# Local attention and a squared-ReLU layer on one core: bias put into the score banks first, masks made at the start, two more tiles transposed by DMA

## The chip, the cores and the metric

The kernel runs on one core of a Trainium2 chip. The metric is device time in microseconds (us) of one launch; several runs are taken and their median is compared. One execution is also recorded by the hardware profiler; its views show each engine's instructions by start time and line of the kernel, counted from the first instruction. Engines: PE (TensorE, matmuls; PEld is its weight load), ACT (ScalarE), DVE (VectorE), POOL (GpSimd), SP (SyncE). POOL and SP start transfers (DMA); their queues are called POOLq and SPq.

## The reference

Attention over 4 batches of 8 heads, 768 positions, head size 64. Each position sees the 96 latest positions, itself included, and the first 8 ("global") ones. A linear bias by distance, with a slope for each head, is added. The result goes through a two-layer network.

```python
scores = scale * np.matmul(q, k.transpose(0, 1, 3, 2))
rel = pos[:, None] - pos[None, :]
is_global = pos[None, :] < int(n_global)              # 8
is_local = (rel >= 0) & (rel < int(n_local))          # 96
dist = np.where(is_global & ~is_local, float(n_local), np.abs(rel))
scores = np.where(is_global | is_local, scores - slopes * dist, -1e9)
a = softmax(scores);  x = a @ v       # x: 3072 rows, 8 heads * 64 = 512 columns
h = x @ w_in                          # 512 -> 2048
out = np.maximum(h, 0.0) ** 2 @ w_out # 2048 -> 512
```

## The kernel before, in words

**Tiles.** The 3072 rows are 24 tiles of 128 rows (index `j`), six to a batch. Because 96 is less than 128, a tile attends to itself and to the tile before it; the eight global keys and values are copied into the first rows of the neighbour (L524 for k, L595 for v). The first tile of a batch attends only to itself. Two tiles are a block of the network (12 blocks).

**Attention of a tile.** q and k arrive with rows on the partitions and must be transposed. For tiles 0 to 5 PE does it (L376; tile 0 in fp32, since it is loaded by SP without a cast, the others in bf16), and ACT or DVE copies the result from PSUM (L305 or L307, whichever the planner picks). From tile 6 on (`JQK`) a DMA transpose on SP does it (L400). Scores are matmuls of L435 with 64 rows of weights. How bias and mask come in depends on the tile. For tiles 0 to 2 (`NBIAS`), PE adds them by further matmuls into the same PSUM banks, after the scores (L447): the weights are identities scaled by the head's slope (`sid`), the moving operand is a 128 x 256 table of distances and masks (`pb`, for first tiles `pb0`). ACT then takes the exponential of the banks (L483). From tile 3 on ACT takes the exponential of the bare scores, and DVE multiplies it by a precomputed mask `E` (L508; `E0` for the first tile of a batch), which ACT makes as exp(slope * pb) by eight instructions of L313. L550 multiplies by v; DVE divides by the row sums (L577, L578) and leaves `x`. x has to be transposed for the network: up to tile 5 by PE (L613) and a copy (L305 or L307), from tile 6 on (`JX`) by a DMA transpose on SP (L637), which waits for x.

**Network.** A block has eight steps. Step s: `hT` = w_in slice times x transposed (L661, 8 matmuls), ACT's ReLU (L682), DVE's square (L694, 14 buffers), then two sums into the two accumulator banks (L731, 2 matmuls each). After eight steps the sums are copied out and stored by SP (L766).

**Constants.** DVE clears a zero tile and writes ones; POOL makes position differences `pbi` by an iota (L244); DVE derives two identities (L255, L256), `pbt`, `pbw`, `pb` (L259 to L265), eight `sid` (L267), then `pb0` and the rows of global keys (L270 to L274). PE runs eight matmuls on zeros first (L254).

**Loads.** POOL issues nearly all loads (L193), with a cast to bf16, in a fixed order: q of tile 1, k of tile 1, v of tiles 0 and 1, then tiles 2 to 5 among the sixteen slices of w_in and w_out. Tiles from 6 on are loaded into two buffers by turns, when the transpose of the tile two before has freed them.

**Order.** Everything after the constants is an operation of a planner (class `Plan`): it has a cost for each engine that could do it, dependencies, a key (lower goes first among operations that can start at about the same time), and may take buffers of a ring. `run` simulates the engines with these costs and `LAG` (the time from the end of an operation until another engine can use its result) and emits the instructions in the order of the simulated starts. On the chip each engine then keeps that order and waits where data is not there. Six PSUM banks are such a ring (`G`): transposes, scores, `hT` and most products with v take its banks in turn; an operation that takes a bank waits until the users of that bank, six allocations ago, have finished.

Of the kernel before, what the change touches and what calls it, by code (L numbers as in the profile page):

```python
# [11 lines left out]
FP32 = mybir.dt.float32  # L12
# [9 lines left out]
class Plan:  # L22
# [8 lines left out]

    LAG = {"PE": 0.25, "ACT": 0.15, "DVE": 0.12, "SP": 2.6, "POOLQ": 0.8, "DMAQ": 1.2, "DMA": 0.0}
    URGE = 0.05
# [66 lines left out]
def kernel(  # L100
# [36 lines left out]
    NBIAS = 3  # L137
    JQK, JX = 6, 6
    NQ, NKT = 2, 2 * TPB
# [32 lines left out]
    NHS = 14  # L172
    E_AT = 14.0
    NWARM = 8
# [65 lines left out]
    nc.vector.memset(zero.bitcast(I32), 0)  # L240
    for j in range(NFIRST + 2):
        nc.vector.memset(v_sb[j][:, :, D : D + 1], 1.0)
    load_part(0, 1)
    nc.gpsimd.iota(pbi, pattern=[[-P, 2], [-1, P]], base=0, channel_multiplier=1)  # L244
    issue[0] += 0.4
    load_part(1, 1)
# [6 lines left out]
    for i in range(NWARM):  # L253
        nc.tensor.matmul(out=warm, lhsT=zero[:, :P], rhs=zero, start=True, stop=True)  # L254
    nc.vector.tensor_scalar(ident32, pbi[:, 0, :], 0.0, None, op0=Alu.is_equal)  # L255
    nc.vector.tensor_scalar(ident, pbi[:, 0, :], 0.0, None, op0=Alu.is_equal)  # L256

# [5 lines left out]
        pbw, pbi, float(n_local - 1), -MASK_VAL, op0=Alu.add, op1=Alu.mult  # L263
    )
    nc.vector.tensor_tensor(out=pb, in0=pbt, in1=pbw, op=Alu.min)  # L265
    for h in range(H):
        nc.vector.tensor_scalar_mul(sid[h], ident, float(slopes[h] / scale))  # L267

    def emit_pb0(e):
        nc.vector.tensor_copy(pb0, pb[:, 0, :])  # L270
        nc.vector.tensor_scalar_max(
            pb0[:n_global, :], pb0[:n_global, :], float(-n_local)
        )
        nc.vector.memset(pb[:n_global, 1, :], float(-n_local))  # L274

    pb_op = plan.op(("pb",), {"DVE": 0.75}, emit_pb0, key=-40.0)

    def emit_ones(e, js):
        for j in js:
            nc.vector.memset(v_sb[j][:, :, D : D + 1], 1.0)  # L280

# [21 lines left out]
    def any_copy(e, dst, src):  # L303
        if e == "ACT":
            nc.scalar.copy(dst, src)  # L305
        else:
            nc.vector.tensor_copy(dst, src)  # L307

    maskE = [
        plan.op(  # L310
            ("E", odd, g), {"ACT": 0.8}, key=0.3 + 2 * g + odd, ready=E_AT,
            emit=lambda e, odd=odd, g=g: [
                nc.scalar.activation(  # L313
                    E[:, odd, g, i], pb, Act.Exp, scale=float(slopes[4 * g + 2 * i + odd])
                )
                for i in range(2)
            ],
        )
        for g in range(2)
        for odd in range(2)  # L320
    ]

    def emit_E0(e, odd):
# [7 lines left out]
        plan.op(  # L331
            ("E0", odd), {"DVE": 0.6}, emit=lambda e, odd=odd: emit_E0(e, odd), key=9 + odd,
            deps=[maskE[odd], maskE[2 + odd]],
        )
# [11 lines left out]
    for j in range(NT):  # L346
# [22 lines left out]
        for n in range(2) if j < JQK else ():  # L369
            users = []  # L370

            def emit_tr(e, j=j, n=n, fp=fp):
                tr = ps_g.tile([P, NPAIR, P], FP32 if fp else BF16, name="tr", tag="g")
                src = plain[n, j] if fp else qk_ring[slot(j)][:, n, :]
                for pair in range(NPAIR):
                    nc.tensor.transpose(  # L376
                        out=tr[:, pair, :], in_=src[:, pair * P : (pair + 1) * P],
                        identity=ident32 if fp else ident,
                    )
                tiles["tr", n, j] = tr  # L380

            tr = plan.op(
                ("tr", n, j), {"PE": 0.5 if fp else 0.24}, emit_tr,
                deps=[land["qk"[n], j]], key=base, takes=(*G, [users]),
            )

            def emit_T(e, j=j, n=n, T_=T_):
                any_copy(e, T_[:, n], tiles.pop(("tr", n, j)))

            c = plan.op(  # L390
                ("T", n, j), {"DVE": 0.7 if fp else 0.43, "ACT": 0.57}, emit_T,
                deps=[tr] + ku, key=base + 0.1,
            )
            users += [tr, c]
            parts.append(c)
            if not fp:
                qk_users[slot(j)].append(tr)
# [20 lines left out]

        def emit_sc(e, gs, j=j, first=first):
            sc = {}  # L420
            for g in gs:
                for odd in range(2):
                    sc[odd, g] = ps_g.tile([P, 4, P], FP32, name="sc", tag="g")
                    tiles["sc", j, odd, g] = sc[odd, g]
            todo = [
                (0, pair, pair, 0) if first else (pair // 2, pair, 2 * (pair % 2) + kt, kt)
                for pair in range(NPAIR)
                for kt in range(1 if first else 2)
            ]
            todo = [x for x in todo if x[0] in gs]  # L430
            opened = set()
            for g, pair, at, kt in todo:
                for odd in range(2):
                    half = slice(odd * D, (odd + 1) * D)
                    nc.tensor.matmul(  # L435
                        out=sc[odd, g][:, at, :],
                        lhsT=qkT[(j - kt) % NKT][half, 1, pair, :],
                        rhs=qkT[j % NKT][half, 0, pair, :],

                        start=j >= NBIAS or (odd, g) not in opened,  # L440
                        stop=j >= NBIAS,
                        skip_group_check=True,
                    )
                    opened.add((odd, g))
            for g, pair, at, kt in todo if j < NBIAS else ():
                for odd in range(2):
                    nc.tensor.matmul(  # L447
                        out=sc[odd, g][:, at, :],
                        lhsT=sid[2 * pair + odd],
                        rhs=pb0 if first else pb[:, kt, :],  # L450
                        start=False,
                        stop=True,
                        skip_group_check=True,
                    )

        deps = list(parts)
        if j < NBIAS:
            deps.append(pb_op)
        if not first:
            deps += tiles["kready", j - 1] + [glob.get(("k", j - 1))]  # L460
        s_ = {}
        for gs in [(0,), (1,)] if j < NSPLIT and not first else [tuple(range(groups))]:
            n = 8 * len(gs)
            o = plan.op(
                ("sc", j, gs[0]), {"PE": 0.25 + 0.029 * n + (0.056 * n if j < NBIAS else 0)},
                lambda e, gs=gs, f=emit_sc: f(e, gs), deps=deps, key=base + 1 + 2 * gs[0],
                takes=(*G, busers[2 * gs[0] : 2 * gs[-1] + 2]),
            )
            ku.append(o)
            if not first:  # L470
                kT_users[(j - 1) % NKT].append(o)
            s_.update({g: o for g in gs})
        for g in range(groups):
            for odd in range(2):
# [3 lines left out]
                def emit_exp(e, j=j, odd=odd, g=g):  # L478
# [10 lines left out]
                x_ = plan.op(  # L489
                    ("exp", j, odd, g), {"ACT": 0.58}, emit_exp, deps=[s_[g]],  # L490
                    key=base + 1.1 + 2 * g + odd,
                    takes=("at", 8, [musers]) if j < NBIAS else ("esc", 3, [eusers]),
                )
                users += [s_[g], x_]
                if j < NBIAS:
# [5 lines left out]
                def emit_mul(e, j=j, odd=odd, g=g, first=first):  # L501
# [9 lines left out]
                m_ = plan.op(  # L511
                    ("mul", j, odd, g), vec(0.38), emit_mul,
                    deps=[x_, maskE0[odd] if first else maskE[2 * g + odd]],
                    key=base + 1.2 + 2 * g + odd, takes=("at", 8, [musers]),
# [7 lines left out]
        if 1 <= t < TPB - 1:  # L522
            def emit_gk(e, j=j, t=t):
# [4 lines left out]
            glob["k", j] = plan.op(  # L528
                ("gk", j), vec(0.17), emit_gk, deps=list(s_.values()), key=base + 4
            )  # L530
# [6 lines left out]
        for hf in range(2):  # L537
# [34 lines left out]
            def emit_norm(e, j=j, hf=hf):  # L572
# [12 lines left out]
            n_ = plan.op(  # L585
                ("norm", j, hf), vec(0.6), emit_norm,
                deps=[p_] + norm, key=base + 2.3 + 2 * hf,
# [5 lines left out]
        if 1 <= t < TPB - 1:  # L593
            def emit_gv(e, j=j, t=t):
                nc.vector.tensor_copy(v_sb[j][:n_global], v_sb[j - t][:n_global])  # L595

            glob["v", j] = plan.op(
                ("gv", j), vec(0.28), emit_gv, deps=[p_, norm[1]], key=base + 5
            )
# [6 lines left out]
        if j < JX:  # L606
# [22 lines left out]

            c = plan.op(("xT", j), {"DVE": 0.43, "ACT": 0.57}, emit_xT, deps=[f_], key=base + 5.1, takes=xT_ring)  # L630
            users += [f_, c]
# [22 lines left out]
    for n, (blk, s) in enumerate(order1):  # L654
# [30 lines left out]
        rusers = []  # L685
        r = plan.op(("relu", blk, s), {"ACT": 0.58}, emit_relu, deps=[a], key=n + 0.5, takes=("hr", 2, [rusers]))
        users.append(r)
# [8 lines left out]

        d = plan.op(("sq", blk, s), vec(0.68), emit_sq, deps=[r], key=n + 1.0, takes=("hs", NHS, [husers]))
        rusers.append(d)
# [10 lines left out]
    for blk in range(NBLK):  # L709
# [9 lines left out]
        for s, sub, half in order2:  # L719
# [29 lines left out]
            if s == NSTEP - 1:  # L749
                ousers = []  # L750

                def emit_o(e, blk=blk, sub=sub, half=half, cols=cols):
# [4 lines left out]
                ev = plan.op(  # L757
                    ("o", blk, sub), {"ACT": 0.57, "DVE": 0.62} if half is None else {"ACT": 0.37},
                    emit_o, deps=[o], key=8 * blk + s + 1.0, takes=("o", 4, [ousers]),
# [16 lines left out]

    for o in plan.run({"PE": 4.2, "DVE": 4.4, "ACT": 4.2, "DMAQ": issue[1]}):
        if o["emit"]:
            o["emit"](o["engine"])
# [35 lines left out]
```

## Time and profile before

| What | Value |
|---|---|
| median of 5 runs | 216.15 us (215.5 to 216.94) |
| the profiled execution: its time / its span | 216.94 us / 215.1 us |
| last matmul ends | 212.0 us |
| PE / DVE / ACT / POOL busy | 206.1 / 142.0 / 118.8 / 73.9 us |
| granted TensorE clock | 1.000 |
| idle of PE before its first matmul | 1.19 us |
| PE busy from 7.7 to 15.6 us | 6.73 of 7.90 us |
| PE busy from 15.6 to 28.1 us | 11.35 of 12.50 us |
| PE busy from 28.1 to 68.7 us | 40.54 of 40.60 us |
| PE busy from 68.7 to 212.0 us | 142.37 of 143.30 us |
| packet time of POOL's load queue / of SP's queue, share of 16 DMA engines | 84.0% / 33.9% |

A line of a timeline gives the start, the duration, the engine, the line of the kernel, the output and inputs, the shape and the count, and in brackets the idle time of the engine just before it with what ended it. A line of the waits gives the waiting instruction, what it waited for, the total in us, the number of waits and the longest. PE's matmuls overlap in the pipeline, so the time a group costs is read from one start to the next.

### The profile page before, as it was taken

Reading aid. Unit: us, or ns where it says so; the run is one execution under the profiler, and the core shown is the slowest. Engines: PE = TensorE matmul, PEld = TensorE weight load, DVE = VectorE, ACT = ScalarE, POOL = GpSimd, SP = SyncE. Lnnn points to the kernel's source line nnn. Section 1 sums busy time; section 2 is a strip of 40 time slices with the busy share of each in tenths; the row PEclk is TensorE's granted clock in tenths of the full one; section 3 lists DMA queues with packets and bytes.
Section 4 is the critical chain, followed back from the end, with each engine's and each line's share of the span. In section 5 each row is a group of like instructions: output and inputs, shape, how many; then the busy total and the mean of one; then the engine's idle time right before and its main releaser. Section 6 shows DMA issues by size and latency. Waiting matters only on the chain.

```text
span 215.1 us, 5031 instructions
## 1 busy us (share of the span) xinstructions
PE 206.1 (96%) x1992; PEld 141.4 (66%) x1992; DVE 142.0 (66%) x366; ACT 118.8 (55%) x218; POOL 73.9 (34%) x91
## 2 busy tenths in 40 slices
PE   7689999999998999999999999999999999999994
PEld 3576567657665767666767667666767767766773
DVE  5287967735687668657778768666767767755540
ACT  2598675714574735733845745733746746734431
POOL 7996677309044440408143140408112000000000
PEclk9999999999999999999999999999999999999999
DMA  9999999999999999799969959999999810310202
GB/s 127 151 163 198 181 195 184 175 215 108 163 190 111 195 137 118 136 144 96 149 147 117 160 117 118 148 125 108 198 127 84 174 24 3 122 24 3 98 0 98
DMA packets 113702, 27.58 MB, mean 128 GB/s; under 512 B 104336, under 2 KB 110736, under 8 KB 113680
## 3 DMA queue, kind: packets, MB, share of 16 engines
q0 software_dynamic: 79200, 13.37, 84.0%
q1 hardware_dynamic: 34480, 13.90, 33.9%
q8 instruction: 15, 0.25, 0.5%
q14 instruction: 7, 0.06, 0.1%
HBM read 27.26 MB, written 6.29 MB: 156 GB/s over the span
## 4 chain that ended last, share of the span: by engine, by line
PE 66%; DMA 23%; POOL 7%; issue 2%; ACT 0%; POOLq 0%; DVE 0%; SPq 0%
PE hT L661 30%; PE acc L731 29%; DMA qk<-in_k_dram 8%; DMA qkT<-qk 5%; DMA win<-in_moe_w_in_dram 4%; DMA wout<-in_moe_w_out_dram 4%; PE sc L435 4%; POOL qk L193 3%; PE po L550 3%; DMA xT<-x 2%; POOL v L193 2%; POOL win L193 1%; POOL wout L193 1%; ACT o L305 0%; POOL pbi L244 0%
## 5 line engine op out<-in xcount | busy, mean ns | idle before, releaser
L661 PE MATMUL hT<-xT,win 128*128 128x256 bf16 x768 | 99.0, 273 | 1.8 <-DMA xT<-x 0.9
L731 PE MATMUL acc<-wout,hs 128*128 128x512 bf16 (+1 forms) x400 | 95.6, 370 | 0.1
L682 ACT ACTIVATE hr<-hT 128x512 f32<-128x512 f32 x96 | 57.3, 598 | 61.6 <-PE hT L661 60.1
L661 PEld LDWEIGHTS <-win 128*128 128x128 bf16 x768 | 70.9, 98 | 19.9 <-DMA win<-in_moe_w_in_dram 1.6
L694 DVE TENSOR_TENSOR hs<-hr 128x512 bf16<-128x512 f32 x96 | 65.0, 689 | 25.5 <-ACT hr L682 24.8
L731 PEld LDWEIGHTS <-hs 128*128 128x128 bf16 x400 | 38.5, 98 | 27.8 <-DVE hs L694 0.2
L483 ACT ACTIVATE esc<-sc 128x512 bf16<-128x512 f32 x78 | 42.6, 598 | 13.2 <-PE sc L435 13.1
L193 POOL DMA_DIRECT2D qk<-in_q_dram x23 | 20.7, 899 | 82.2 <-DMA qkT<-qk 80.0
L508 DVE TENSOR_TENSOR at<-esc,E 128x512 bf16<-128x512 bf16 x78 | 32.4, 420 | 6.9 <-ACT esc L483 5.8
L193 POOL DMA_DIRECT2D v<-in_v_dram x24 | 21.6, 900 | 2.0 <-DVE at L508 1.2
L578 DVE TENSOR_TENSOR x<-po,rs 128x256 bf16<-128x256 f32 x48 | 20.4, 424 | 1.7
L193 POOL DMA_DIRECT2D qk<-in_k_dram x23 | 20.7, 900 | 1.5 <-DMA v<-in_v_dram 1.3
L550 PEld LDWEIGHTS <-at 128*128 128x128 bf16 x352 | 16.7, 98 | 5.8 <-ACT at L483 0.4
L550 PE MATMUL po<-v,at 128*128 128x65 bf16 x352 | 18.7, 193 | 0.3 <-ACT at L483 0.3
L435 PEld LDWEIGHTS <-qkT 64*128 64x128 bf16 x352 | 9.9, 94 | 9.9 <-issue 8.3
L577 DVE RECIPROCAL rs<-po 128x4 f32<-128x4 f32 x48 | 8.7, 181 | 9.7 <-PE po L550 9.6
L435 PE MATMUL sc<-qkT 64*128 64x128 bf16 x192 | 13.2, 219 | 1.0 <-DVE qkT L307 0.5
L305 ACT COPY o<-acc 128x512 f32<-128x512 f32 (+1 forms) x14 | 7.8, 557 | 9.2 <-PE acc L731 9.2
L307 DVE COPY o<-acc 128x512 f32<-128x512 f32 x11 | 7.6, 692 | 7.2 <-PE acc L731 7.2
L435 PE MATMUL sc<-qkT,qkT 64*128 64x128 bf16 x160 | 11.4, 216 | 0.0
L524 DVE COPY qkT<-qkT 128x32 bf16<-128x32 bf16 x16 | 3.6, 227 | 7.4 <-PE sc L435 7.3
L193 POOL DMA_DIRECT2D win<-in_moe_w_in_dram x8 | 6.5, 811 | 0.6 <-DMA wout<-in_moe_w_out_dram 0.6
(40 smaller groups left out, 60.4 us busy)
## 6 DMA issues: line engine op xcount, KB each, us to landing
out_dram<-o SPq DMA_DIRECT2D x23, 256.0 KB, 3.7
v<-in_v_dram POOLq DMA_DIRECT2D x24, 128.0 KB, 6.4
qk<-in_q_dram POOLq DMA_DIRECT2D x23, 128.0 KB, 4.9
qk<-in_k_dram POOLq DMA_DIRECT2D x23, 128.0 KB, 5.7
win<-in_moe_w_in_dram POOLq DMA_DIRECT2D x8, 256.0 KB, 8.5
wout<-in_moe_w_out_dram POOLq DMA_DIRECT2D x8, 256.0 KB, 8.8
qkT<-qk SPq DMA_TRANSPOSE x18, 5.0
xT<-x SPq DMA_TRANSPOSE x18, 3.1
```

The costliest lines, as they stand in the source:

```text
L193: nc.gpsimd.dma_start(out=dst, in_=src)
L305: nc.scalar.copy(dst, src)
L435: nc.tensor.matmul(out=sc[odd, g][:, at, :], lhsT=qkT[(j - kt) % NKT][half, 1, pair, :], rhs=qkT[j % NKT][half, 0, pair, :],  start=j >= N ...
L483: nc.scalar.activation(out=esc, in_=tiles.pop(("sc", j, odd, g)).rearrange("p a c -> p (a c)"), func=Act.Exp, scale=scale,)
L508: nc.vector.tensor_mul(at, tiles.pop(("esc", j, odd, g)), bias)
L550: nc.tensor.matmul(out=po[:, hi, :], lhsT=tiles["at", j, odd, g][:, at * P : (at + 1) * P], rhs=v_sb[kj][:, h, :], start=(i == 0), stop=(i ...
L577: nc.vector.reciprocal(rs, po[:, :, D : D + 1])
L578: nc.vector.tensor_tensor(out=x[:, 4 * hf : 4 * hf + 4, :], in0=po[:, :, :D], in1=rs.to_broadcast([P, 4, D]), op=Alu.mult,)
L661: nc.tensor.matmul(out=hT[:, c, :], lhsT=w_in_sb[s][:, kt, c * P : (c + 1) * P], rhs=tiles["xT", blk][:, kt, :], start=(kt == 0), stop=(kt ...
L682: nc.scalar.activation(hr, tiles.pop(("hT", blk, s)), Act.Relu)
L694: nc.vector.tensor_mul(hs, hr, hr)
L731: nc.tensor.matmul(out=tiles["acc", blk, sub, half], lhsT=hs[:, c, sub * P : (sub + 1) * P], rhs=w_out_sb[s][:, c, cols], start=(s == 0 an ...
```

## The change

1. *Bias first.* For tiles 0 to 2 the bias matmuls become an operation of their own (`bias`). It depends on the tile's second transpose (`tr`, that of k), takes the PSUM banks and opens them (`start`); the scores depend on it and add to the banks.
2. *Constants.* The iota goes ahead of POOL's first load. The identities move behind `pbt` and `pbw`; `pb0` and the rows of global keys come before the `sid`, outside the planner. The eight instructions that make `E` on ACT come right after these, before everything that the planner orders; before, they were four operations of the planner, not to start before 14 us of its time. `E0` then waits for nothing but a planned time of 8.0.
3. *x by DMA.* `JX` goes from 6 to 4: x of tiles 4 and 5 is transposed on SP too, so 20 tiles instead of 18.
4. *The planner's numbers.* Lags of ACT and DVE, the costs of many operations, and the times at which engines are free at the start.

```diff
-    LAG = {"PE": 0.25, "ACT": 0.15, "DVE": 0.12, "SP": 2.6, "POOLQ": 0.8, "DMAQ": 1.2, "DMA": 0.0}
+    LAG = {"PE": 0.25, "ACT": 0.26, "DVE": 0.2, "SP": 2.6, "POOLQ": 0.8, "DMAQ": 1.2, "DMA": 0.0}
...
-    JQK, JX = 6, 6
+    JQK, JX = 6, 4
...
-    E_AT = 14.0
...
+    nc.gpsimd.iota(pbi, pattern=[[-P, 2], [-1, P]], base=0, channel_multiplier=1)
     load_part(0, 1)
-    nc.gpsimd.iota(pbi, pattern=[[-P, 2], [-1, P]], base=0, channel_multiplier=1)
-    issue[0] += 0.4
     load_part(1, 1)
...
-    nc.vector.tensor_scalar(ident32, pbi[:, 0, :], 0.0, None, op0=Alu.is_equal)
-    nc.vector.tensor_scalar(ident, pbi[:, 0, :], 0.0, None, op0=Alu.is_equal)
...
+    nc.vector.tensor_scalar(ident32, pbi[:, 0, :], 0.0, None, op0=Alu.is_equal)
+    nc.vector.tensor_scalar(ident, pbi[:, 0, :], 0.0, None, op0=Alu.is_equal)
     nc.vector.tensor_tensor(out=pb, in0=pbt, in1=pbw, op=Alu.min)
+
+    nc.vector.tensor_copy(pb0, pb[:, 0, :])
+    nc.vector.memset(pb[:n_global, 1, :], float(-n_local))
+    nc.vector.tensor_scalar_max(pb0[:n_global, :], pb0[:n_global, :], float(-n_local))
     for h in range(H):
         nc.vector.tensor_scalar_mul(sid[h], ident, float(slopes[h] / scale))
...
+    for g in range(2):
+        for odd in range(2):
+            for i in range(2):
+                nc.scalar.activation(
+                    E[:, odd, g, i], pb, Act.Exp, scale=float(slopes[4 * g + 2 * i + odd])
+                )
...
-            ("E0", odd), {"DVE": 0.6}, emit=lambda e, odd=odd: emit_E0(e, odd), key=9 + odd,
-            deps=[maskE[odd], maskE[2 + odd]],
+            ("E0", odd), {"DVE": 0.62}, emit=lambda e, odd=odd: emit_E0(e, odd), key=9 + odd,
+            ready=8.0,
...
-                ("T", n, j), {"DVE": 0.7 if fp else 0.43, "ACT": 0.57}, emit_T,
+                ("T", n, j), {"DVE": 0.61 if fp else 0.41, "ACT": 0.48}, emit_T,
...
+        def emit_bias(e, gs, j=j, first=first, todo=todo, open_sc=open_sc):
+            open_sc(gs)
             opened = set()
+            for g, pair, at, kt, odd in todo(gs):
+                nc.tensor.matmul(
+                    out=tiles["sc", j, odd, g][:, at, :],
+                    lhsT=sid[2 * pair + odd],
+                    rhs=pb0 if first else pb[:, kt, :],
+                    start=(odd, g) not in opened,
+                    stop=False,
+                    skip_group_check=True,
+                )
+                opened.add((odd, g))
+
+        def emit_sc(e, gs, j=j, todo=todo, open_sc=open_sc):
+            if j >= NBIAS:
+                open_sc(gs)
+            for g, pair, at, kt, odd in todo(gs):
+                half = slice(odd * D, (odd + 1) * D)
+                nc.tensor.matmul(
+                    out=tiles["sc", j, odd, g][:, at, :],
+                    lhsT=qkT[(j - kt) % NKT][half, 1, pair, :],
+                    rhs=qkT[j % NKT][half, 0, pair, :],
+                    start=j >= NBIAS,
+                    stop=True,
+                    skip_group_check=True,
+                )
...
+            takes = (*G, sc_users)
+            bias = None
+            if j < NBIAS:
+                bias = plan.op(
+                    ("bias", j, gs[0]), {"PE": 0.056 * n},
+                    lambda e, gs=gs, f=emit_bias: f(e, gs), deps=[tr],
+                    key=base + 0.9 + 2 * gs[0], takes=takes,
+                )
+                takes = None
             o = plan.op(
-                ("sc", j, gs[0]), {"PE": 0.25 + 0.029 * n + (0.056 * n if j < NBIAS else 0)},
-                lambda e, gs=gs, f=emit_sc: f(e, gs), deps=deps, key=base + 1 + 2 * gs[0],
-                takes=(*G, busers[2 * gs[0] : 2 * gs[-1] + 2]),
-            )
+                ("sc", j, gs[0]), {"PE": 0.2 + 0.029 * n},
+                lambda e, gs=gs, f=emit_sc: f(e, gs), deps=[*deps, bias],
+                key=base + 1 + 2 * gs[0], takes=takes,
+            )
...
-                    ("exp", j, odd, g), {"ACT": 0.58}, emit_exp, deps=[s_[g]],
+                    ("exp", j, odd, g), {"ACT": 0.48}, emit_exp, deps=[s_[g]],
...
-        d = plan.op(("sq", blk, s), vec(0.68), emit_sq, deps=[r], key=n + 1.0, takes=("hs", NHS, [husers]))
+        d = plan.op(("sq", blk, s), vec(0.61), emit_sq, deps=[r], key=n + 1.0, takes=("hs", NHS, [husers]))
...
-    for o in plan.run({"PE": 4.2, "DVE": 4.4, "ACT": 4.2, "DMAQ": issue[1]}):
+    for o in plan.run({"PE": 4.2, "DVE": 4.2, "ACT": 5.3, "DMAQ": issue[1]}):
```

`open_sc` takes the PSUM tiles of the scores; `todo` lists a tile's score matmuls by group, pair of heads, place, key tile and head of the pair. Further costs change in the same way: ReLU from 0.58 to 0.48, the mask's product from 0.38 to 0.34, the division from 0.6 to 0.55, the copies of k's and v's global rows from 0.17 to 0.1 and 0.28 to 0.25, the copies of the sums from 0.57 and 0.62 to 0.48 and 0.61.

## The prediction

> **What bounds the kernel now.** I read the times first: the profiled execution took 216.94 us around a span of 215.1 us, so 1.84 us lie outside the span. The median of the five runs is 216.15 us; I do the sums in the trace and take them off the median. Then the busy shares: TensorE (PE) works 96% of the span, the next engine 66%. Then PE's list of waits, which tells what a change can win at most:
>
> ```profile
> PE 206.1 (96%) x1992; PEld 141.4 (66%) x1992; DVE 142.0 (66%) x366; ACT 118.8 (55%) x218; POOL 73.9 (34%) x91
> ```
>
> ```profile
> PE tr L376 <- DMA plain<-in_k_dram: 0.9, 1, 0.9
> PE hT L661 <- DMA xT<-x: 0.9, 1, 0.9
> PE hT L661 <- DMA win<-in_moe_w_in_dram: 0.7, 2, 0.4
> PE sc L435 <- DVE qkT L307: 0.5, 1, 0.5
> PE sc L435 <- ACT qkT L305: 0.5, 1, 0.5
> PE trx L613 <- DVE x L578: 0.4, 1, 0.4
> PE po L550 <- ACT at L483: 0.3, 1, 0.3
> ```
>
> Each line gives the total, the number and the longest of one kind of wait. Up to its last matmul at 212.0 us PE idles 5.9 us in all; these lines and 1.2 us before the first matmul are most of it. Then the stages: from 28.1 to 68.7 us PE is busy 40.54 of 40.60 us, from 70 to 205 us without a gap. So a gain can come from PE work that disappears, or from idle time before 28 us (and the 0.9 us at 69.6 us). Last, PE's timeline of the first tiles, with start, duration and, in brackets, the idle time ahead:
>
> ```profile
> 6.34 0.66 PE L376 MATMUL tr<-ident,plain 128*128 128x128 f32 x4 [0.92 <-DMA plain<-in_k_dram]
> 6.84 0.39 PE L376 MATMUL tr<-ident,qk 128*128 128x128 bf16 x4
> 7.68 0.40 PE L435 MATMUL sc<-qkT 64*128 64x128 bf16 x8 [0.45 <-ACT qkT L305]
> 8.01 0.62 PE L447 MATMUL sc<-pb,sid 128*128 128x128 bf16 x8
> 8.47 0.39 PE L376 MATMUL tr<-ident,qk 128*128 128x128 bf16 x4
> 9.37 0.23 PE L435 MATMUL sc<-qkT 64*128 64x128 bf16 x2 [0.52 <-DVE qkT L307]
> ```
>
> PE transposes k, idles while ACT or DVE copies the transpose out, then does scores (L435) and only then the bias (L447), although the bias needs neither q nor k.
>
> **Part 1, bias ahead of the scores (tiles 0 to 2).** The same 40 matmuls, 8 for tile 0 and 16 each for tiles 1 and 2. Eight take 0.46 us of PE order (8.01 to 8.47). For tile 0 they fit the 0.45 us gap at 7.23; for tile 1 the first eight fit the 0.52 us gap at 8.85. That is 0.45 + 0.45 = 0.90 us. The second eight of tile 1 win nothing I count. Tile 2 had gaps of 0.25 (at 12.34, for an exp on ACT) and 0.40 (at 13.28, for x on DVE). Its transposes at 11.86 and 12.78 hang on loads issued at 6.06 and 6.94, which don't come earlier, but its bias now lies beside the copy of k. Bounds 0 and 0.90; I take the nearest gap, 0.40. Part 1: 1.30 us. New wait: a bias waits for the second transpose of its tile, for constants, and for two PSUM banks of a ring of six; behind it in PE's order stand its own scores. Tile 1's second bias needs the banks of two earlier users, at the latest an exp of tile 0 that ends near 8.7 us, so it can't come first.
>
> **Part 2, constants and masks at the start.** POOL: the iota (0.37 us) goes past the load of q of tile 1, which began at 1.25 us. Between 0.64 and 1.25 us POOL ran nothing, so the load is late by 0 to 0.37 us, and the loads behind it are early by up to the same. Its q is transposed at 6.84; the median q load takes 4.9 us, so it lands at 6.15 to 6.52. No cost. DVE: pbi is there at 1.1 to 1.7 instead of 2.71. The five operations from pbi to pb took 2.75 to 4.05 us, 1.30 by starts; copy, memset and maximum 0.45 + 0.17 + 0.18; eight sid 0.93 by starts. From 1.4 to 1.7 on: pb is final at 3.3 to 3.7, the sid end at 4.5 to 4.8, ahead of the first transpose's end at 5.43 and the bias at 7.2. The identities move behind two operations (0.34 + 0.35), still ready before 4.58. ACT: eight masks, four of which took 1.33 us, so 2.66 us, from 3.3 to 3.7 until 6.0 to 6.4. What stands behind them on ACT is tile 0's copies; the q copy (ACT, 5.47) goes to DVE or waits, and the k copy at 7.04 is the one that the scores wait for. Cover 0.6 us; if the masks end after 7.04, all that follows is late by the excess. What they free is ACT time at 13.69 to 15.02, 19.01 and 22.56, and E0 on DVE (1.2 us) can move too. DVE and ACT have room, so I count 0 here; at most the 0.7 us for win and the 0.4 in small waits go, if work of block 1 comes early enough to fill them.
>
> A row about DVE beside POOL: the eight sid operations take 177 to 586 ns each while POOL writes loads. [...]
>
> **Part 3, x of tiles 4 and 5 by DMA.** PE loses two groups of four transposes, 36.10 to 36.32 and 45.38 to 45.61: 0.45 us, all on the path, since PE is busy throughout. ACT loses 0.59 and DVE 0.42, off the path. SP gains two issues of 1.19 us each, and the DMA engines two transposes. Landing takes:
>
> ```profile
> qkT<-qk SPq DMA_TRANSPOSE x18, 5.0
> xT<-x SPq DMA_TRANSPOSE x18, 3.1
> ```
>
> The range for x is 2.4 to 6.4 us. In DMA time, the SP queue has 33.9% of 215.1 = 72.9 us; 18 transposes of x and 18 of qk, twice as large, make 54 units, so one of x costs at most 1.35 us, at least 0. Tile 5's x is done at 44.26, so its transpose lands at 46.7 to 50.7. Who waits? Eight steps of L661 per block: the last steps of block 1 are the groups at 46.47, 48.21 and 50.38, so block 2 starts at 52.24, or 50.5 with a gain of 1.75 in front. Cover 3.1 us at the median, none at 6.4. New wait on SP: the issue stands until x is normalised, and behind it stand the qk transposes of tiles 6 and 7 (43.14, 45.62) and the stores. Tile 6 landed at 48.15 and its scores ran at 49.18, cover 1.0. I take 0.2 us lost, near the bottom of 0 to 2.3, because PE has sums of block 1 (L731) to do meanwhile.
>
> [...]
>
> **The planner's numbers.** New costs and lags (ACT 0.58 to 0.48, its lag 0.15 to 0.26) issue nothing but reorder. From 70 us on PE has no gap that an order could fill: nothing counted, bounds -0.9 (the gap at 69.6 closes) to +0.9 (it doubles).
>
> **Sum.** 0.90 + 0.40 + 0.45 - 0.20 = 1.55 us. Span 215.1 to 213.55; the profiled execution 216.94 to 215.39; the median 216.15 to **214.6 us**. Unknowns of tile 2 and the loss give this case 213.9 to 215.0. A measurement here tells about 0.5%, 1.08 us, from no change.
>
> **Rivals.**
> *More (0.14):* the win waits, the small waits and the one at 69.6 us go as well, 0.7 + 0.4 + 0.9 less what stays: 2.8 to 3.3 us in all, about 213.0. For it: ACT is free in 13 to 23 us, so tile 3 is done sooner. Against: the win loads land when they land.
> *Eaten (0.26):* the gain in front is given back at arrivals that don't move: win (19.33, 24.56), tile 4's k (27.56), the qk transpose of tile 6 (48.15), x of tile 7 (landing at 69.56). Then 0.45 us of transposes and little else stays: about 215.7. The same time results if the bank ring keeps the bias from going ahead.
> *Slower (0.20):* SP's queue. If the transpose of x of tile 5 stands ahead of tile 6's qk and waits for x until 44.26, tile 6 is issued at 44.26 + 1.19 = 45.45 instead of 43.14 and lands at 50.5, with a share of the engines at 51.5. Its scores, and block 2 behind them, are then up to 51.5 - 49.18 = 2.3 us late, and everything won before is lost in that wait: 216.5 to 218.5, about 217.4. Above 50.26 us for the landing it is slower by over 0.5%. Against: block 1's backlog can go first.
>
> **Numbers.** My forecast 0.40, more 0.14, eaten 0.26, slower 0.20. Faster: 0.40 + 0.14 + 0.02 of the third = 0.56; same 0.24; slower 0.20. Range 212.9 to 217.3: it takes in "more" and the lower half of "slower".
>
> **What would show it.** Right: L447's matmuls ahead of L435's, no gap of 0.45 and 0.52 us before the first scores, the first exp at 8.2 instead of 8.61; masks on ACT done by 7.0; 16 matmuls of L613, 20 transposes of x on SP; PE's last matmul near 210.4. Wrong: a copy of k of tile 0 that starts after 7.04; PE waits on a transpose from SP between 45 and 53 us; PE waits for win longer than 0.7 us; a gap at 69 us that has grown.

## The result and the profile after

The changed kernel takes 217.17 us (median; 216.07 to 220.45), the kernel before 216.26 us beside it. The ratio is 1.0037, with an interval of 1.0021 to 1.0052: slower by 0.8 us, where the prediction had 1.55 us faster. The two profiled executions alone would mislead: the changed kernel's took 216.31 us with a span of 214.5 us, and the 216.94 us of the other lies 0.7 us above its own median. So below I also use a second profile of each kernel (`b_again`, span 213.8 us, and `a_again`, 215.2 us). Five of the changed kernel's 44 executions with a clock on record, 1.5% and more above its fastest, are left out of the ratio. Of the other 39, 16 had a mean granted TensorE clock below 0.997 and a median of 217.30 us; 23 had 0.997 or more and a median of 216.90. Of the kernel before, 116 of 129 executions with a clock on record had 0.997 or more, with a median of 216.2 us. So about 0.7 us of the loss stand without a lowered clock; the clock falls more often in the changed kernel, but it doesn't make most of the loss.

TensorE's share first. It is what it was, with 8 matmuls fewer: the transposes of x of tiles 4 and 5 (L613 had 24, L612 has 16):

```profile
PE 206.3 (96%) x1984; PEld 143.0 (67%) x1984; DVE 142.8 (67%) x366; ACT 117.1 (55%) x216; POOL 74.4 (35%) x91
```

Then its list of waits (total, number, longest), below the 1.2 us ahead of its first matmul:

```profile
PE sc L436 <- DMA qkT<-qk: 1.1, 1, 1.1
PE tr L360 <- DMA qk<-in_k_dram: 0.5, 1, 0.5
PE sc L436 <- ACT qkT L303: 0.5, 1, 0.5
PE tr L360 <- DMA qk<-in_q_dram: 0.4, 1, 0.4
```

The waits for copies ahead of the scores of tiles 0 and 1 are gone; the wait for a copy in the third line belongs to tile 3, which has no bias matmuls (its scores start at 19.79). The first line is new: scores that wait for a DMA transpose of q and k. In the second profile of the same kernel this line reads 2.9 us in 2 waits. The front of TensorE's timeline:

```profile
6.43 0.61 PE L420 MATMUL sc<-pb,sid 128*128 128x128 bf16 x8
...
7.27 0.40 PE L436 MATMUL sc<-qkT 64*128 64x128 bf16 x8
...
7.83 0.61 PE L420 MATMUL sc<-pb,sid 128*128 128x128 bf16 x8
8.51 0.23 PE L436 MATMUL sc<-qkT 64*128 64x128 bf16 x2
...
12.01 0.40 PE L360 MATMUL tr<-ident,qk 128*128 128x128 bf16 x4 [0.43 <-DMA qk<-in_q_dram]
12.90 0.61 PE L360 MATMUL tr<-ident,qk 128*128 128x128 bf16 x4 [0.50 <-DMA qk<-in_k_dram]
```

Bias (L420) stands ahead of scores (L436), the two gaps are filled, and tile 1's scores start at 8.51 instead of 9.37. At 12 us TensorE meets q and k of tile 2, which land when they land. Now SyncE's queue, where the loss comes from. Each line is a group of issues; the second column is the time from the first issue to the end of the last. Before:

```profile
43.14 1.38 SPq L400 DMA_TRANSPOSE qkT<-qk  x1
...
45.62 9.50 SPq L400 DMA_TRANSPOSE qkT<-qk  x2
56.54 1.19 SPq L637 DMA_TRANSPOSE xT<-x  x1
```

After:

```profile
37.09 8.08 SPq L636 DMA_TRANSPOSE xT<-x  x2
45.29 3.60 SPq L384 DMA_TRANSPOSE qkT<-qk  x2
48.94 5.18 SPq L765 DMA_DIRECT2D out_dram<-o  x4
55.03 1.62 SPq L636 DMA_TRANSPOSE xT<-x  x1
56.76 5.81 SPq L384 DMA_TRANSPOSE qkT<-qk  x2
```

The first group of two after is x of tiles 4 and 5. Its second member stands until 45.17 us, and the q and k transpose of tile 6 behind it is issued at 45.29, not 43.14. It lands at 50.25 instead of 48.15. GpSimd's timeline shows what hangs on it, the load of tile 8, which takes over tile 6's buffers. Before, then after:

```profile
48.72 0.88 POOL L193 DMA_DIRECT2D qk<-in_q_dram  x1 [8.03 <-DMA qkT<-qk]
```

```profile
50.82 0.87 POOL L192 DMA_DIRECT2D qk<-in_q_dram  x1 [10.18 <-DMA qkT<-qk]
```

The load starts 2.1 us later. Tile 8's k lands at 56.21 instead of 53.81. Its transpose was issued at once before (the second member of the group from 45.62, at 53.88). Now it stands behind four stores and x of tile 6, is issued at 56.76 and lands at 63.20 instead of 58.81: 4.4 us later. Of these 2.1 are the load's start, 0.3 more go by until k has landed, 0.5 are the place behind x of tile 6, and 1.5 a longer flight, in which block 1's stores and x of tile 6 land first. Before, TensorE did those scores without a wait; now it reaches them at 62.2 us and waits. Before, then after:

```profile
62.92 0.23 PE L435 MATMUL sc<-qkT 64*128 64x128 bf16 x2
```

```profile
63.25 0.23 PE L436 MATMUL sc<-qkT 64*128 64x128 bf16 x2 [1.06 <-DMA qkT<-qk]
```

Here is the same loss as a table. It gives the start of each block's first group of L661 (L660 after) and the end of the last matmul, in us. The order of other work differs a little between the plans, so it shows a direction, not a balance.

| profile | block 1 | block 2 | block 3 | end |
|---|---|---|---|---|
| before | 32.63 | 52.24 | 69.61 | 211.97 |
| before, second profile | 32.62 | 51.97 | 68.28 | 210.63 |
| after | 31.16 | 51.07 | 68.63 | 210.98 |
| after, second profile | 30.03 | 51.01 | 69.35 | 211.70 |

At 30 us the changed kernel is 1.5 to 2.6 us ahead. At 51 us about 1 us of it is left, and at 69 us no gain can be told. From block 3 on, every one of these takes 142.35 us.

### The profile page after: what moved, and what is told of

Read it like the earlier page. It is cut to its first block, busy times and chain, and to the rows that moved or that the text cites. A ratio compares the mean times of both kernels' runs of the same rounds, so it can differ in the third digit from the quotient of the medians.

```text
span 214.5 us, 5021 instructions
## 1 busy us (share of the span) xinstructions
PE 206.3 (96%) x1984; PEld 143.0 (67%) x1984; DVE 142.8 (67%) x366; ACT 117.1 (55%) x216; POOL 74.4 (35%) x91
## 4 chain that ended last, share of the span: by engine, by line
PE 86%; DMA 6%; ACT 3%; POOL 3%; DVE 1%; issue 0%; SPq 0%; POOLq 0%; ACTq 0%
PE acc L730 37%; PE hT L660 37%; PE sc L436 5%; PE po L549 4%; DMA qkT<-qk 3%; DMA qk<-in_k_dram 3%; POOL qk L192 1%; POOL v L192 1%; ACT at L482 1%; PE sc L420 1%; ACT esc L482 1%; PE tr L360 1%; ACT hr L681 1%; POOL win L192 0%; DVE hs L693 0%
## 5 line engine op out<-in xcount | busy, mean ns | idle before, releaser
L660 PE MATMUL hT<-xT,win 128*128 128x256 bf16 x768 | 98.5, 273 | 0.0
L730 PE MATMUL acc<-wout,hs 128*128 128x512 bf16 (+1 forms) x400 | 97.6, 370 | 0.0
L660 PEld LDWEIGHTS <-win 128*128 128x128 bf16 x768 | 73.0, 98 | 22.8
L693 DVE TENSOR_TENSOR hs<-hr 128x512 bf16<-128x512 f32 x96 | 65.8, 686 | 21.4 <-ACT hr L681 19.7
L730 PEld LDWEIGHTS <-hs 128*128 128x128 bf16 x400 | 36.5, 98 | 24.3 <-DVE hs L693 0.2
L192 POOL DMA_DIRECT2D v<-in_v_dram x24 | 22.3, 931 | 2.3 <-DVE hs L693 1.2
L436 PEld LDWEIGHTS <-qkT 64*128 64x128 bf16 x352 | 10.3, 96 | 10.2 <-issue 7.2
L436 PE MATMUL sc<-qkT 64*128 64x128 bf16 x192 | 13.5, 222 | 1.6 <-DMA qkT<-qk 1.1
L436 PE MATMUL sc<-qkT,qkT 64*128 64x128 bf16 x160 | 11.6, 220 | 0.0
L482 ACT ACTIVATE at<-sc 128x512 bf16<-128x512 f32 x10 | 5.3, 597 | 3.9 <-PE sc L436 3.8
L192 POOL DMA_DIRECT2D wout<-in_moe_w_out_dram x8 | 5.8, 727 | 2.8 <-DMA win<-in_moe_w_in_dram 1.5
```

Source lines behind the costliest of these rows:

```text
L192: nc.gpsimd.dma_start(out=dst, in_=src)
L436: nc.tensor.matmul(out=tiles["sc", j, odd, g][:, at, :], lhsT=qkT[(j - kt) % NKT][half, 1, pair, :], rhs=qkT[j % NKT][half, 0, pair, :], s ...
L482: nc.scalar.activation(out=esc, in_=tiles.pop(("sc", j, odd, g)).rearrange("p a c -> p (a c)"), func=Act.Exp, scale=scale,)
L660: nc.tensor.matmul(out=hT[:, c, :], lhsT=w_in_sb[s][:, kt, c * P : (c + 1) * P], rhs=tiles["xT", blk][:, kt, :], start=(kt == 0), stop=(kt ...
L693: nc.vector.tensor_mul(hs, hr, hr)
L730: nc.tensor.matmul(out=tiles["acc", blk, sub, half], lhsT=hs[:, c, sub * P : (sub + 1) * P], rhs=w_out_sb[s][:, c, cols], start=(s == 0 an ...
```

## Experiments

Three explanations stood at the start: transposes that arrive late (by the added DMA work or by the order of SyncE's queue), the planner's new numbers, and TensorE's own work and clock. The ratio is to the kernel before, run beside each. `order` is the order in which instructions are issued; an entry moved in it is the same instruction at another place of its engine's queue. T stands for the q and k transpose by DMA, xT for that of x, st for a store; T(6) is that of tile 6.

**The kernels once more** (`b_again`, `a_again`: no edit).

> The kernel before once more, for a second profile of it. Its profiled execution of 216.94 us was slow beside its median of 216.26 us. If the 0.9 us wait at 69.6 us for x of tile 7 is typical, it is there again; if it was bad luck, PE's last matmul ends near 211.2 us instead of 212.0 and the wait is under 0.3 us.

> The changed kernel once more, for a second profile. Theory SP order: the transpose of x of tile 5 goes ahead of tile 6's qk transpose on SP, which is issued at about 45.3 us instead of 43.1; tile 8's scores wait about 1 us near 63 us again. Theory clock: the clock falls to 0.5 between 13 and 16 us again, which costs about 1.5 us; without it PE is 1.5 us further at 17 us.

215.77 and 217.04 us. The first has no wait on a DMA transpose in 44 to 69 us, the second has two for T(6) and T(8):

```profile
50.24 0.40 PE L436 MATMUL sc<-qkT 64*128 64x128 bf16 x8 [1.01 <-DMA qkT<-qk]
63.97 0.23 PE L436 MATMUL sc<-qkT 64*128 64x128 bf16 x2 [1.84 <-DMA qkT<-qk]
```

**The planner's numbers alone, on the kernel before** (`b_num`; all costs and lags of the diff, without the times at which engines are free at the start).

```diff
-    LAG = {... "ACT": 0.15, "DVE": 0.12, ...}
+    LAG = {... "ACT": 0.26, "DVE": 0.2, ...}
...
```

> The kernel before with the planner's new costs and lags alone. SP's order stays as before: qk of tile 6, then stores; qk of tile 8 ahead of x of tile 6. Theory SP order (the loss is that x transposes stand ahead of qk transposes): 0.995 to 1.000 of before, the scores of tile 8 don't wait. Theory planner's numbers (the new costs give a worse order by themselves): 1.003 or more.

0.9995 (0.9964 to 1.0026): nothing, as counted.

**Part 3 alone, on the kernel before** (`b_jx4`).

```diff
-    JQK, JX = 6, 6
+    JQK, JX = 6, 4
```

> The kernel before with JX at 4 alone; the planner keeps qk of tile 6 ahead of x of tile 5 and qk of tile 8 ahead of x of tile 6. Theory SP order: 0.997 to 0.999, PE saves 0.45 us. Theory DMA share (two more transposes beside the last loads make k of tile 6 land at 44.6 instead of 43.1 us, as in the swapped kernel): qk of tile 6 is issued at 44.3 or later, the chain behind it is late, 1.001 to 1.004.

1.0068 (1.0038 to 1.0098): 1.5 us slower, although TensorE does 0.45 us less. The route is another than in the changed kernel: this plan has T(6) ahead of xT(5) and T(8) ahead of xT(6), and though T(6) lands at 49.0 (47.77 and 48.15 in the two profiles before), T(8) lands at 59.4, in time. Late is x of tile 7, which is issued at 64.5 and lands at 70.6, after 6.1 us (before 5.0 and 3.6). Block 3 waits for it:

```profile
70.73 1.03 PE L661 MATMUL hT<-xT,win 128*128 128x256 bf16 x8 [2.15 <-DMA xT<-x]
```

**Part 3 taken back** (`a_jx6`), and **parts 1 and 2 alone** (`a_oldnum_jx6`, which also has the old costs and lags).

```diff
-    JQK, JX = 6, 4
+    JQK, JX = 6, 6
```

> The changed kernel with JX back at 6, so x of tiles 4 and 5 is transposed by PE (the planner orders anew). Theory SP order: tile 6's transpose is issued near 43.1 us, PE does 0.45 us more, and the time is 0.995 to 0.999 of the kernel before. Theory clock or theory planner's numbers: 1.003 to 1.006, the loss lies in the other parts.

> The changed kernel with the planner's old numbers and JX at 6: what stays of the change is the bias ahead of the scores and the constants and masks at the start. Theory SP order: SP's order is as before (qk of tile 8 ahead of x of tile 6), 0.994 to 0.998. Theory clock and start (loads 0.25 us later, waits for q and k of tile 2 near 12 us, clock at half speed after them in half of the executions): 1.001 to 1.004, with a mean clock of 0.99 in some executions.

1.0068 (1.0027 to 1.0109) and 1.0025 (0.9986 to 1.0065). Neither gains. In the first, the new plan puts xT(6) ahead of T(8), which is issued at 57.4 and lands at 62.9. In the second the queue is nearly that of before; T(8) lands at 60.2 in time, but x of tile 7, issued at 63.9, lands at 69.8:

```profile
PE hT L660 <- DMA xT<-x: 1.9, 1, 1.9
```

So parts 1 and 2 alone win at the front and meet a wait of 1.9 us ahead of block 3.

**Bias of tile 2 ahead of its q transpose** (`a_b2move`).

```diff
+    # entry ("bias", 2, 0) moved ahead of ("tr", 0, 2) in order
```

> The changed kernel with one operation moved in the emitted order: the first half of tile 2's bias (8 matmuls) goes ahead of the transpose of tile 2's q, into PE's idle time near 11.5 us. Theory clock: PE idles 0.45 us less between 10.5 and 13 us, executions with a mean clock under 0.995 become rare (before the change none, in the changed kernel about half), and the time falls by 0.3 to 0.5 us, to about 1.002. Theory SP order: the time stays within 0.2 us of the changed kernel, because PE waits later anyway for qk of tiles 6 and 8.

1.0046 (1.0009 to 1.0084), the changed kernel's own loss: with the bias in the gap at 12 us the kernel still waits for T(6) (0.97) and T(8) (2.12).

**T(6) ahead of xT(5)** (`a_swap`), **T(8) ahead of block 1's stores and xT(6)** (`a_t8only`), **both** (`a_t8st`), all on the changed kernel.

```diff
-    for o in plan.run({...}):
+    order = plan.run({...})
+    for a, b in ((("T", 6), ("xT", 5)), (("T", 8), ("st", 1, 0))):
+        names = [o["name"] for o in order]
+        o = order.pop(names.index(a))
+        order.insert([o["name"] for o in order].index(b), o)
+    for o in order:
```

> The changed kernel with one pair swapped in the emitted order: tile 6's qk transpose ahead of the transpose of x of tile 5. Theory SP order: tile 6's transpose is issued near 43.1 us, the load of tile 8 starts near 48.8 instead of 50.8, the wait of tile 8's scores goes, and the time falls by about 1 us, to 0.998 to 1.000 of the kernel before. Theory clock: nothing changes, 1.003 to 1.004. Theory that block 2's x is now late: PE waits for x of tile 5 near 51 us and the time stays or grows.

> The changed kernel with one entry of SyncE's queue moved: the q and k transpose of tile 8 ahead of block 1's stores and of the x transpose of tile 6. Tile 6's transpose stays behind that of x of tile 5. If tile 8's place carries the loss, this is near the kernel with both moves (0.9971): 0.997 to 0.999. If tile 6's place carries it, since load 8 waits for it, it stays near the changed kernel: 1.001 to 1.004.

> The changed kernel with two entries of SyncE's queue moved up: the q and k transpose of tile 6 ahead of the x transpose of tile 5, and that of tile 8 ahead of the two stores of block 1 and of the x transpose of tile 6. Same work everywhere. Theory A with the queue's order as the cause: tile 8's transpose is issued as soon as its q and k are loaded, some 2 us earlier, lands near 61 us, and the kernel is some 1 us faster (ratio to before 0.998 to 1.000). Theory A with the DMA engines' load as the cause: the transpose is issued earlier and lands no earlier, or x of tile 6 or 7 lands later by as much; time within 0.3 us of the changed kernel. Theory B: no change.

1.0018 (0.9985 to 1.0052), 1.0006 (0.9973 to 1.0038), and 0.9971 (0.9951 to 0.9992). Moving two entries of one queue turns 0.8 us slower into 0.6 us faster, with the same instructions: in the profiles of the changed kernel and of `a_t8st` every engine but SyncE has the same work in the same order. The clock doesn't explain it either: at 0.997 or more the median is 215.27 us, against 216.90. Each entry alone gives a part; by the intervals they can't be ranked. SyncE's queue with both moved:

```profile
44.08 1.23 SPq L384 DMA_TRANSPOSE qkT<-qk  x1
45.36 1.28 SPq L636 DMA_TRANSPOSE xT<-x  x1
...
55.09 1.25 SPq L384 DMA_TRANSPOSE qkT<-qk  x1
```

The line from 55.09 is T(8), ahead of the stores (56.43) and xT(6) (57.94). It lands at 60.5, no scores wait for a transpose, and x of tile 7 (67.6) is the next to come last:

```profile
67.71 1.03 PE L660 MATMUL hT<-xT,win 128*128 128x256 bf16 x8 [1.01 <-DMA xT<-x]
```

**Four more warm-up matmuls** (`a_warm12`), to see whether TensorE's time at the front counts at all.

```diff
-    NWARM = 8
+    NWARM = 12
```

> The changed kernel with twelve warm-up matmuls in place of eight: four more of 0.43 us or so start (8 took 3.59 us with their tail), so TensorE's first transposes, biases and scores come 1.2 to 1.7 us later; no transfer is touched. If arrivals up to block 3 set the time (theory A), what TensorE loses at the front is taken out of its later waits: the scores of tile 8 still wait for a transpose that lands at 63 to 64 us, block 3 starts at the 68.6 to 69.5 us of before, and the time changes by 0.3 us at most. If TensorE's own work sets it (theory B), block 3 and the end come 1.2 to 1.7 us later, a ratio near 1.010 to 1.012 against before.

1.0145 (1.0102 to 1.0189), 2.3 us slower than the changed kernel. The ratio says less than it seems: four of the six executions had a mean clock of 0.992 or less, and the two at 1.000 took 217.49 and 218.23 us, 0.6 and 1.3 us above the changed kernel's 216.90. Theory A held that arrivals up to block 3 stand still. In the profile (218.23 us) they don't: T(8) landed at 65.1, 1.2 to 1.9 us later than in the two profiles of the changed kernel, and k of tile 6 at 45.1 (43.8 and 44.3). GpSimd's queue shows the lateness early. The load of v of tile 4, with all loads in line behind it, is issued at 21.00 here, at 20.18 and 20.22 in the two profiles of the changed kernel:

```profile
21.00 0.88 POOL L192 DMA_DIRECT2D v<-in_v_dram  x1 [0.95 <-DVE hs L693]
```

The profile names VectorE as what ended the wait. That can't be read as it stands, since this load is emitted ahead of all that the planner orders, L693 included. In all 20 profiles it starts 0.94 or 0.95 us after the third slice of w_in has landed, which GpSimd issued near 12 us. That slice landed at 20.06 here and at 19.24 in the changed kernel's profile, but at 20.15 and 20.40 in `a_front_x7` and `a_t8_jx6`, which have eight warm-up matmuls. So the late loads here needn't come from the delay at the front, and the run doesn't settle between theories A and B.

**q and k of tiles 6 and 7 by TensorE**, on the changed kernel (`a_jqk8`) and on the kernel before (`b_jqk8`).

```diff
-    JQK, JX = 6, 4
+    JQK, JX = 8, 4
```

> The changed kernel with q and k of tiles 6 and 7 transposed by TensorE instead of by DMA: 16 more matmuls and four copies, two DMA transposes of 256 KB or so fewer, and no transpose on the way between the load of tile 6 and that of tile 8. Theory A: load 8 starts 1 to 2 us earlier, tile 8's transpose lands near 60 us, block 3 starts 1 to 2 us earlier, and the kernel gets faster by 0.5 to 1.5 us in spite of TensorE's added 0.9 us. Theory B: TensorE's added work shows in full, 0.9 us slower.

> The kernel before with the same edit (q and k of tiles 6 and 7 transposed by TensorE). It still transposes x of tiles 4 and 5 on TensorE, so more of the early work lies there. Theory A: the arrivals ease, the time stays within 0.5 us or falls. Theory B: 0.9 us slower (ratio 1.004).

1.0139 (1.0103 to 1.0175) and 1.0036 (1.0010 to 1.0063). The second agrees with TensorE's added work and no more: where nothing waited for T(6), taking it off the DMA wins nothing. The first was a miss for both theories: it is 2.2 us slower than the changed kernel (1.7 us by the medians at a clock of 0.997 or more, 218.62 and 216.90), where A had it faster and B 0.9 us slower. Its trace, of the slowest of its six executions (221.26 us), has the same fault in a worse form. T(8) stands behind four stores and xT(6), is issued at 56.22 though its k landed at 53.34, and flies 7.3 us:

```profile
54.92 1.19 SPq L636 DMA_TRANSPOSE xT<-x  x1
56.22 6.55 SPq L384 DMA_TRANSPOSE qkT<-qk  x2
```

**x of tile 7 by TensorE.** This takes the last arrival away from block 3: on the kernel before (`b_x7`); on parts 1 and 2 with the old numbers, x of tiles 4 and 5 on TensorE and T(8) ahead of block 1's stores (`a_front_x7`); and on the changed kernel with both entries moved (`a_t8_x7`).

```diff
-        if j < JX:
+        if j < JX or j == 7:
```

> The kernel before with x of tile 7 transposed by TensorE: the wait of 0 to 0.9 us ahead of block 3 goes, 0.25 us of TensorE comes. Expected: 0.997 to 1.000.

> Part 1 and 2 of the change alone (bias ahead of the scores, masks and constants moved; the old planner numbers, x of tiles 4 and 5 by TensorE), with SyncE's queue in the order of the kernel before and with x of tile 7 transposed by TensorE. If the front gain of 0.9 us is real and only an arrival (x of tile 7) ate it in the same kernel without that edit (1.0025), it shows now against the kernel before with that edit: 0.8 to 1.0 us faster than it. If the front gain is lost earlier, at the loads of tiles 2 and 3 or at the weights, both are equal.

> The changed kernel with the reordered queue (tile 6's transpose ahead of x of tile 5, tile 8's ahead of block 1's stores) and x of tile 7 transposed by TensorE in place of a DMA transpose: 8 more matmuls and a copy, no wait of block 3 for a landing. If x of tile 7 was what block 3 waited for last, it starts 0.8 us or so earlier, ratio 0.993 to 0.995. If something else stands just behind (tile 8's transpose, the hidden activations, TensorE's own work), 0.997 to 0.999.

1.0014 (0.9991 to 1.0037), 0.9976 (0.9954 to 0.9997) and 0.9930 (0.9902 to 0.9958). On the kernel before it wins nothing; one of that kernel's two profiles waits there (0.9 us), the other doesn't. Between the first two lie parts 1 and 2 alone: 0.0038 or 0.8 us (with both half-widths added in squares, 0.1 to 1.5). So the front gain is real, and in `a_oldnum_jx6` it was the arrival of x of tile 7 that ate it.

**x of tiles 4 and 5 back on TensorE, with the queue mended** (`a_t8_jx6`), and **all of it** (`a_t8_jx6_x7`: also x of tile 7).

```diff
-    JQK, JX = 6, 4
+    JQK, JX = 6, 6
...
+    # entry ("T", 8) moved ahead of ("st", 1, 0) in order
```

> The changed kernel with x of tiles 4 and 5 transposed by TensorE again (no added DMA transposes; 16 matmuls back) and the transpose of tile 8 issued ahead of block 1's stores and of the x transpose of tile 6, as in the kernel before. If the order of SyncE's queue was the whole cost, this is slower than the reordered changed kernel (0.9971) by the 0.45 us of the matmuls: ratio 0.998 to 1.000. If the two added DMA transposes cost something of their own (1 us each on a backlogged engine), it is faster than that: 0.992 to 0.996. If x of tile 7 is the arrival that then decides, block 3 waits 1 to 2 us for it and the ratio is 1.000 to 1.003.

> The changed kernel with all that the runs point to: tile 8's transpose ahead of block 1's stores and of x of tile 6, x of tiles 4 and 5 back on TensorE and x of tile 7 there too. Against the version that keeps x of tiles 4 and 5 on DMA (0.9930): if the two DMA transposes cost about what they save TensorE, the two are equal, 0.991 to 0.995. If they still load the way to tile 8, this one is faster, 0.988 to 0.991.

0.9963 (0.9934 to 0.9991) and 0.9910 (0.9880 to 0.9941). Against their twins with x of tiles 4 and 5 on DMA (0.9971, 0.9930) the differences are 0.0008 and 0.0020, inside the intervals. So with the queue in order, part 3 is worth nothing that could be told here: its 0.45 us of TensorE doesn't show, and no run tells where it goes. The last has the lowest ratio of all, 1.9 us below the kernel before (interval 1.3 to 2.6). Its waits hold no transpose by DMA any more:

```profile
PE tr L360 <- DMA qk<-in_q_dram: 0.8, 1, 0.8
PE tr L360 <- DMA qk<-in_k_dram: 0.5, 1, 0.5
```

## Why the prediction was wrong

**Bias ahead of the scores, 0.90 for tiles 0 and 1: right in mechanism and size.** Both gaps are gone, the first exp starts at 7.70 (forecast 8.2, before 8.61), and parts 1 and 2 alone give 0.8 us (0.1 to 1.5) where nothing eats it. **Tile 2's 0.40 didn't come.** The gaps for ACT and DVE were replaced by waits for q and k of tile 2, 0.43 and 0.50, whose landing (12.0 and 12.9 us; 11.4 and 12.2 before) the prediction named as fixed and then did not let bind. In the second profile the waits there are 0.25 for ACT and 0.49 for k.

**Constants and masks, 0: right.** The eight masks end at 5.88 us, ahead of the copy of k that the scores need:

```profile
3.32 2.56 ACT L276 ACTIVATE E<-pb 128x256 bf16<-128x256 bf16 x8 [1.09 <-DVE pb L269]
6.63 0.59 ACT L303 CAST qkT<-tr 128x512 bf16<-128x512 f32 x1 [0.75 <-PE tr L360]
```

On GpSimd the prediction had the loads behind the iota "early by up to the same". They are 0.25 us later (5.58 for win instead of 5.32), since the two loads of v take longer. Before, then after:

```profile
3.58 1.76 POOL L193 DMA_DIRECT2D v<-in_v_dram  x2
```

```profile
3.22 2.38 POOL L192 DMA_DIRECT2D v<-in_v_dram  x2
```

VectorE's eight sid operations now run from 3.40 to 4.70, beside them; but before, the same eight ran from 4.05 to 5.39, beside the same two loads, and these took 1.76 us. New beside the loads are ScalarE's masks. No run isolates what made the loads longer.

**The first step that failed is part 3's term for SyncE's queue:** "I take 0.2 us lost, near the bottom of 0 to 2.3, because PE has sums of block 1 (L731) to do meanwhile". The order of that queue cost 1.4 us (1.0037 to 0.9971 with two entries moved; 0.9 to 2.0 with both half-widths added in squares). The prediction's reason was true and beside the point. TensorE did have sums to do: in the profiled execution it ran 26 matmuls of L730 in one piece until 50.30 and took T(6), landed at 50.25, without a gap. But the late T(6) releases the load of tile 8 late. I followed the delay to the scores of tile 6 and not along the buffers to T(8), the next link. On the kernel before, part 3 costs 1.5 us net, so some 1.95 us are lost against the 0.45 won, but at x of tile 7 and not at T(8); and taking it back alone (`a_jx6`) didn't mend the changed kernel. So the term belongs to the order of the queue in the whole plan, not to part 3 by itself.

**The second is the sum: 0.90 and 0.40 were counted in full to the end.** Parts 1 and 2 alone measured 1.0025 (0.9986 to 1.0065), where 1.30 us faster would be 0.994. Their profile shows why: block 3 waits 1.9 us for x of tile 7, landed at 69.8. The prediction named this arrival in its rival "eaten" and put no term for it into the sum.

**The rival "slower" had the place, the time and nearly the price.** It had T(6) issued at 45.45 and landing at 50.5, measured 45.29 and 50.25; it gave 217.4 us, measured 217.17. I gave it 0.20 on the ground that "block 1's backlog can go first". The price is near in part by luck: it was for scores of tile 6 that wait up to 2.3 us, and they waited 0 and 1.01 us in the two profiles, while the scores of tile 8 waited 1.06 and 1.84. What the rival lacked is the second entry: in the new plan T(8) stands behind block 1's stores and xT(6), which the prediction didn't ask.

**The planner's numbers, 0:** right by themselves on the kernel before. But with the bias in, the new plan gives another order of SyncE's queue than the old one (`a_jx6` puts T(8) behind xT(6), `a_oldnum_jx6` ahead of it), so "issue nothing but reorder" was no ground for 0. What that order costs by itself isn't shown: 1.0068 and 1.0025 have intervals that overlap.

Of the signs named beforehand, the front's were met, the first exp 0.5 us earlier than named; TensorE's last matmul came at 210.98 and 211.70 instead of 210.4. Of the wrong ones, a wait on a transpose between 45 and 53 us is there in the second profile (1.01) and not in the first, and none foresaw the wait at 63 us.

**What the runs don't settle.** Which of the two entries costs more; why a transpose of x of tile 7 lands 3.6 us after its issue in one kernel and 6.1 in another; what part 3's transposes cost where the queue is in order; and whether a delay at the front reaches the loads.

## What to carry to other kernels

A gain at the front of a pipeline lasts only up to the next arrival that doesn't move with it: list the arrivals with the time that they land and the time that they are wanted (in the second profile of the kernel before 47.8 and 48.9, 58.4 and 62.7, 67.9 and 68.3), and count no more than the slack allows. When DMA work is added to a queue that issues in order, as SyncE's did here (k of tile 6 landed at 44.27, but T(6) was issued at 45.29, after xT(5) had stood until 45.17), ask for each entry behind it which buffer its landing frees and which load waits for that, one link further than the first consumer. When a change loses where its parts should win, move the late entry forward before taking a part out: two moved entries were worth 1.4 us, and taking part 3 back alone won nothing.

## What the hardware showed

**With a transpose under way on SyncE's queue, a load of GpSimd's landed later.** Tile 6's q and k were issued on GpSimd's queue at the same times as before (33.83 and 34.74; 33.87 and 34.77), and k landed at 44.27 instead of 43.05, with x of tile 4, issued on SyncE at 37.09, landing at 44.02 between them. In the ten profiles with x of tile 4 transposed by DMA this load of k took 9.05 to 9.89 us to land, in the ten without 8.24 to 8.78. The median times to landing over the whole kernel hide this:

```profile
xT<-x SPq DMA_TRANSPOSE x20, 3.8
qkT<-qk SPq DMA_TRANSPOSE x18, 4.4
```

xT(4) took 6.9 us, xT(6) 7.2 and T(8) 6.5, where the cover was needed.

**TensorE's granted clock fell to a half for 3.4 us after short waits, but not each time.** In the changed kernel's profile idle times of 0.18, 0.43 and 0.50 us from 11.0 to 12.9 us are followed by a granted clock of 0.50 from 12.9 to 16.3; the columns are the stretch, its length, the busy times of PE, PEld, DVE, ACT and POOL, then the clock, the DMA's share and its rate:

```profile
12.00:13.00 1.00, 0.49 (x6) 0.32 (x7) 0.48 (x2) 0.56 (x1) 1.00 (x2) 0.95 1.62 153
13.00:14.00 1.00, 1.00 (x11) 1.00 (x12) 0.42 (x1) 0.03 (x1) 1.00 (x3) 0.50 1.77 181
...
16.00:17.00 1.00, 1.00 (x17) 0.84 (x14) 0.48 (x11) 0.78 (x2) 0.43 (x2) 0.84 1.80 177
```

The same stretch of the second profile, with waits of 0.25 and 0.49, kept a clock of 1.00. In `a_jqk8` a wait of 2.21 us at 63.6 was followed by half clock from 64.2 to 67.7, while a wait of 1.84 us in `a_again` was not. So it doesn't hang on the length of the last wait alone; what sets it isn't shown.
